# The end of a fused attention and gMLP kernel: flag read ahead of the last stage, last tile stored in one piece, output tiles finished beside every second step

## Chip, cores, metric

One core of one Trainium2 chip. The metric is the device time in microseconds (us), median over runs. Before: 1325.91 us (3 runs, 1325.71 to 1326.42); with three more runs 1325.83 us (6 runs, 1325.55 to 1326.42).

The profile's names: PE is TensorE, PEld its weight loads, DVE VectorE, ACT ScalarE, POOL GpSimd, SP SyncE; a q behind a name is the sequencer of that engine, under which the profile records its branches, semaphore waits and DMA issues. L1435 is line 1435 of the kernel; the lines after the change are numbered a little lower. Below, an engine's *silence* is the time from the end of its branch record to its next record, its *report* is the start of that next record, and a tile has *landed* where SP's wait record for it starts. *Fetch* is used for what fills a silence, as far as instruction packets in the DMA records show it. The records of these packets name a queue and no engine; they are given to engines here by size and order (in the changed kernel one of 16 KB starts 1.18 us after the start of TensorE's branch, one of 8 KB 1.02 us after DVE's and one 0.94 us after ACT's).

## The reference, cut to what matters

The whole computes adaLN modulation, attention with 32 query heads on a cached K and V of 8 heads, and a spatial-gating MLP. Only the last part is touched:

```python
z = gelu(einsum('bsd,df->bsf', h, w_in))
z1, z2 = z[..., :Fh], layernorm(z[..., Fh:])
g = einsum('ts,bsf->btf', w_sp, z2) + b_sp[None, :, None]
x = x + gb * einsum('bsf,fd->bsd', z1 * g, w_out)      # S = 2048, D = 512, Fh = 896
```

## The kernel before

The fast path computes softmax without subtracting the maximum and then sets `flag` to 0 if all sums were in a safe range. At its end every engine reads the flag into a register and jumps over `general_path`, a complete fallback program, if it is 0 (it is 0 for these inputs). The 2048 rows go in four chunks of 512. In the last chunk the gate is computed in two rounds of seven steps: columns 0 to 383 first, then the last 128 columns. Output tiles 0, 1, 2 of the chunk are complete at step 0 of the second round; tile 3 needs all seven steps.

```python
def finish_tile(t, jj, src, parts=1):
    j = t * CT + jj
    tmp = mlp.tile([P, D], FP32, name="tmp", bufs=2)
    yout = mlp.tile([P, D], BF16, name="yout", bufs=2)
    w = D // parts
    for k in range(parts):
        s = slice(k * w, (k + 1) * w)
        nc.vector.tensor_tensor(out=tmp[:, s], in0=src[:, s], in1=gb_rows[:, s], op=ALU.mult)
        nc.vector.tensor_tensor(out=yout[:, s], in0=tmp[:, s], in1=x_sb[:, j, s], op=ALU.add)
        (nc.scalar, nc.sync)[k].dma_start(out=out_dram[:, j, s], in_=yout[:, s])
# ... cut ...
acc = [bank2(), bank2()]                       # two PSUM tiles of 128 x 1024
o2_last = [acc[jj // 2][:, (jj % 2) * 512 : (jj % 2 + 1) * 512] for jj in range(CT)]
# ... first round, cut ...
for f in range(NFT):                           # second round, NFT = 7 steps
    spatial(last, yT, f, n_a, P, bias_by_pe=True)   # 16 matmuls, 1 bias matmul, 1 gate product on VectorE
    if f == 0:
        for jj in range(CT - 1):
            o2_mm(o2_last[jj], yT, jj, NFT - 1)
    else:
        o2_mm(o2_last[CT - 1], yT, CT - 1, f - 1)
    if 1 <= f < CT:
        finish_tile(last, f - 1, o2_last[f - 1])
o2_mm(o2_last[CT - 1], yT, CT - 1, NFT - 1)
finish_tile(last, CT - 1, o2_last[CT - 1], parts=2)
fast.close()

redo = nc.values_load(flag[0:1, 0:1], min_val=0, max_val=P)
with tc.If(redo != 0):
    general_path(...)
```

Of the kernel before, what the change touches and what calls it, by code (L numbers as in the profile page):

```python
# [13 lines left out]
ALU = mybir.AluOpType  # L14
AX = mybir.AxisListType
P = 128
# [559 lines left out]
def kernel(  # L576
# [19 lines left out]
    nc = tc.nc  # L596
    _, S, D = A_x.shape
# [12 lines left out]
    CT = 512 // P  # L610
# [8 lines left out]
    out_dram = out[0].rearrange("(t p) d -> p t d", p=P)  # L619
# [13 lines left out]
    flag = flagp.tile([1, 1], mybir.dt.int32, name="flag")  # L633
# [12 lines left out]
    x_sb = res.tile([P, NT, D], BF16, name="x_sb")  # L646
    ga_rows = res.tile([P, D], FP32, name="ga_rows")
    gb_rows = res.tile([P, D], FP32, name="gb_rows")
# [14 lines left out]
    def bank(name):  # L663
        return psum.tile([P, 512], FP32, name=name)
# [241 lines left out]
    for k in range(2):  # L906
        ln1_mod(hTs[0][:, k, 0:P], x_ps[0][:, k * P : (k + 1) * P], k)
        nc.scalar.activation(
            out=hTs[0][:, 2 + k, 0:P],
            in_=x_ps[1][:, k * P : (k + 1) * P],  # L910
# [17 lines left out]
    for hf, copy in enumerate((nc.vector.tensor_copy, nc.scalar.copy)):  # L928
        copy(  # L929
            out=qTs[0][:, 2 * hf : 2 * hf + 2, 0:P],  # L930
            in_=q_ps[:, hf * 512 : hf * 512 + 2 * P].rearrange("p (h q) -> p h q", h=2),
# [381 lines left out]
    for f in range(NFT):  # L1313
# [6 lines left out]
        out=ok1[:], in0=rall[:], scalar1=1.0 / SAFE, scalar2=None, op0=ALU.is_ge  # L1320
# [8 lines left out]
        out=bad[:], in0=okm[:], scalar1=-1.0, scalar2=1.0, op0=ALU.mult, op1=ALU.add  # L1329
# [12 lines left out]
    def spatial(t, yT, f, c0, n, bias_by_pe=False):  # L1342

        g_ps = bank("misc")
        cols = slice(t * 512 + c0, t * 512 + c0 + n)
        for st in range(NT):
            nc.tensor.matmul(  # L1347
                g_ps[:, :n],
                lhsT=z2[:, st, f * P : (f + 1) * P],
                rhs=wsp[t][:, st, c0 : c0 + n],  # L1350
                start=(st == 0),
                stop=(st == NT - 1 and not bias_by_pe),
            )
        if bias_by_pe:
            nc.tensor.matmul(  # L1355
                g_ps[:, :n], lhsT=ones_bf[0:1, :], rhs=bsp_bc[0:1, cols], start=False, stop=True
            )
            gbs = g_ps[:, :n]
        else:
            gb = mlp.tile([P, 512], BF16, name="gb", bufs=2)  # L1360
            gbs = gb[:, :n]
            nc.vector.tensor_tensor(out=gbs, in0=g_ps[:, :n], in1=bsp_bc[:, cols], op=ALU.add)  # L1362
        nc.vector.tensor_tensor(
            out=yT[:, f, c0 : c0 + n], in0=gbs, in1=z1T[:, f, cols], op=ALU.mult
        )

    def o2_mm(dst, yT, jj, f):
        nc.tensor.matmul(  # L1368
            dst,
            lhsT=yT[:, f, jj * P : (jj + 1) * P],  # L1370
            rhs=wout_sb[:, f, :],
            start=(f == 0),
            stop=(f == NFT - 1),
        )

    def finish_tile(t, jj, src, parts=1):
        j = t * CT + jj
        tmp = mlp.tile([P, D], FP32, name="tmp", bufs=2)
        yout = mlp.tile([P, D], BF16, name="yout", bufs=2)
        w = D // parts  # L1380
        for k in range(parts):
            s = slice(k * w, (k + 1) * w)
            nc.vector.tensor_tensor(out=tmp[:, s], in0=src[:, s], in1=gb_rows[:, s], op=ALU.mult)
            nc.vector.tensor_tensor(out=yout[:, s], in0=tmp[:, s], in1=x_sb[:, j, s], op=ALU.add)  # L1384
            (nc.scalar, nc.sync)[k].dma_start(out=out_dram[:, j, s], in_=yout[:, s])

    yTs = {}

    def o2_tile(t, jj):
        o2 = bank("o_ps")  # L1390
        for f in range(NFT):
            o2_mm(o2[:], yTs[t], jj, f)
        finish_tile(t, jj, o2)

    last = NCH - 1
    n_a = 512 - P
    for t in range(NCH):
        yTs[t] = mlp.tile([P, NFT, 512], BF16, name="yT", bufs=2)
        if t == last:
            break  # L1400
        for f in range(NFT):
            spatial(t, yTs[t], f, 0, 512)
            if t == 1 and f == CT:
                check_flag()
            if t > 0 and f < CT:
                o2_tile(t - 1, f)
        if t == 0:
            wsp[last] = wspp.tile([P, NT, 512], BF16, name="wsp")
            for st in range(NT):
                load_wsp(wsp[last], last, st)  # L1410
    acc = [bank2(), bank2()]
    o2_last = [acc[jj // 2][:, (jj % 2) * 512 : (jj % 2 + 1) * 512] for jj in range(CT)]
    yT = yTs[last]
    for f in range(NFT):
        spatial(last, yT, f, 0, n_a)
        if f < CT:
            o2_tile(last - 1, f)
        if f > 0:
            for jj in range(CT - 1):
                o2_mm(o2_last[jj], yT, jj, f - 1)  # L1420
    for f in range(NFT):
        spatial(last, yT, f, n_a, P, bias_by_pe=True)
        if f == 0:
            for jj in range(CT - 1):
                o2_mm(o2_last[jj], yT, jj, NFT - 1)
        else:
            o2_mm(o2_last[CT - 1], yT, CT - 1, f - 1)
        if 1 <= f < CT:
            finish_tile(last, f - 1, o2_last[f - 1])
    o2_mm(o2_last[CT - 1], yT, CT - 1, NFT - 1)  # L1430
    finish_tile(last, CT - 1, o2_last[CT - 1], parts=2)
    fast.close()

    redo = nc.values_load(flag[0:1, 0:1], min_val=0, max_val=P)
    with tc.If(redo != 0):  # L1435
        general_path(
            tc, A_x, A_k_cache, A_v_cache, A_wq, A_wo, B_x, B_w_in, B_w_sp, B_b_sp, B_w_out,
# [32 lines left out]
```

## Time and profile before

| kernel before | us | where it is read |
|---|---|---|
| device time, median | 1325.83 | 6 runs |
| span in the profile | 1324.6 | page |
| last bias matmul starts | 1316.09 | timeline, L1355 |
| last VectorE result ends | 1318.81 | timeline, L1384 |
| tail: last bias matmul to end of span | 8.47 | difference, with the end at 1324.56 in the trace |

The profile lines of the kernel before stand in the prediction.

### The profile page before, as it was taken

The numbers are of one execution on the slowest core, as the hardware profiler recorded it, in microseconds if no ns is written. First come the engines' busy times: TensorE is split into PE (matmuls) and PEld (weight loads), VectorE is DVE, ScalarE is ACT, GpSimd is POOL, SyncE is SP. The second block draws the span as 40 slices with busy tenths as digits, with TensorE's granted clock in tenths as the row PEclk, the third lists the DMA queues.
The fourth block names the chain that finished last, engine by engine and source line by source line (L and its number), as shares of the span: only waits on it lengthen the run. The fifth ranks groups of instructions, "written<-read, shape, count | busy, mean of one in ns | idle before, by whom it ended". The sixth has DMA issues, their size and how long they took to land.

```text
span 1324.6 us, 27877 instructions
## 1 busy us (share of the span) xinstructions
PE 1313.2 (99%) x12332; PEld 858.6 (65%) x12332; DVE 473.2 (36%) x1168; ACT 1077.8 (81%) x1061; POOL 49.4 (4%) x92
## 2 busy tenths in 40 slices
PE   8999999999999999999999999999999999999997
PEld 5666666666666666666666666666666666644444
DVE  5632222222222222222222222222222566793444
ACT  6898999999999999999999999999999999650000
POOL 1200000000000000000000000000000000120000
PEclk9999999999999999999999999999999999999999
DMA  7451022102111112111110221021101121143200
GB/s 179 123 122 33 13 49 37 37 13 53 28 26 33 34 37 37 30 36 37 33 37 14 53 37 33 17 52 24 31 13 21 25 34 33 29 116 83 64 21 27
DMA packets 148352, 58.12 MB, mean 44 GB/s; under 512 B 138400, under 2 KB 143904, under 8 KB 148224
## 3 DMA queue, kind: packets, MB, share of 16 engines
q1 hardware_dynamic: 141568, 37.84, 15.1%
q0 software_dynamic: 4208, 16.39, 4.4%
q10 hardware_dynamic: 2448, 2.03, 0.5%
q8 instruction: 98, 1.61, 0.5%
q14 instruction: 30, 0.25, 0.1%
HBM read 21.37 MB, written 2.10 MB: 18 GB/s over the span
## 4 chain that ended last, share of the span: by engine, by line
PE 98%; DMA 0%; DVE 0%; SPq 0%; issue 0%; ACT 0%
PE o_ps L1002 35%; PE s_ps L980 33%; PE misc L1034 8%; PE misc L947 8%; PE misc L1347 7%; PE s_ps L1193 2%; PE s_ps L1232 2%; PE o_ps L1368 1%; PE s_ps L1368 1%; DMA wq_g<-in_A_wq_dram 0%; PE misc L1104 0%; SPq L699 0%; PE misc L1355 0%; PE s_ps L921 0%; PE misc L846 0%; DVE yout L1384 0%
## 5 line engine op out<-in xcount | busy, mean ns | idle before, releaser
L987 ACT ACTIVATE pT<-s_ps 128x1024 bf16<-128x1024 f32 x1024 | 1044.5, 1025 | 83.4 <-PE s_ps L980 9.4
L1002 PEld LDWEIGHTS <-pT 128*128 128x128 bf16 x8192 | 548.5, 98 | 241.2
L1002 PE MATMUL o_ps<-v,pT 128*128 128x129 bf16 x8192 | 631.4, 220 | 0.0
L980 PE MATMUL s_ps<-qT,kT 128*128 128x512 bf16 x2048 | 609.9, 379 | 0.7 <-ACT qT L929 0.7
L1013 DVE RECIPROCAL rall<-o_ps 128x2 f32<-128x2 f32 x256 | 43.7, 171 | 744.4 <-PE o_ps L1002 744.2
L980 PEld LDWEIGHTS <-kT 128*128 128x128 bf16 x2048 | 199.5, 98 | 119.2 <-issue 1.4
L1034 PE MATMUL misc<-wo_g,oT 128*128 128x512 bf16 x512 | 194.0, 379 | 0.0
L947 PE MATMUL misc<-hT,wq_g 128*128 128x512 bf16 (+2 forms) x528 | 189.6, 371 | 0.0
L1014 DVE TENSOR_TENSOR onorm<-o_ps,rall 128x256 bf16<-128x256 f32 x256 | 108.7, 425 | 9.0 <-DVE rall L1013 0.3
L1347 PE MATMUL misc<-wsp,z 128*128 128x512 bf16 (+2 forms) x560 | 100.7, 336 | 0.0
L958 DVE CAST qT<-misc 128x512 bf16<-128x512 f32 x127 | 86.3, 680 | 2.0 <-PE misc L947 1.9
L1347 PEld LDWEIGHTS <-z 128*128 128x128 bf16 x560 | 50.6, 98 | 48.4
L1047 DVE TENSOR_TENSOR xacc<-misc,xacc 128x512 f32<-128x512 f32 x112 | 76.2, 680 | 0.0
L947 PEld LDWEIGHTS <-wq_g 128*128 128x128 bf16 x528 | 50.6, 98 | 1.1 <-issue 0.2
L1034 PEld LDWEIGHTS <-oT 128*128 128x128 bf16 x512 | 50.1, 98 | 0.8
L1362 DVE TENSOR_TENSOR gb<-misc,bsp_bc 128x512 bf16<-128x512 f32 (+1 forms) x28 | 18.4, 658 | 59.0 <-PE misc L1347 59.0
L1193 PE MATMUL s_ps<-win_sb,hT 128*128 128x448 bf16 x128 | 27.0, 352 | 0.0
L1203 ACT ACTIVATE z<-s_ps 128x896 bf16<-128x896 f32 x16 | 14.7, 917 | 14.9 <-PE s_ps L1193 14.9
L1232 PE MATMUL s_ps<-hT,win_sb 128*128 128x512 bf16 x112 | 24.5, 379 | 0.0
L1240 ACT ACTIVATE z1T<-s_ps 128x1024 bf16<-128x1024 f32 x14 | 14.3, 1024 | 10.0 <-PE s_ps L1232 9.1
L691 DVE BATCH_NORM_STATS2 bnst<-x_sb 128x6 f32<-128x512 bf16 x32 | 21.9, 683 | 0.5
L715 POOL DMA_DIRECT2D wq_g<-in_A_wq_dram x7 | 5.3, 753 | 420.9 <-PE misc L947 420.9
(86 smaller groups left out, 283.4 us busy)
## 6 DMA issues: line engine op xcount, KB each, us to landing
wq_g<-in_A_wq_dram POOLq DMA_DIRECT2D x7, 512.0 KB, 3.9
v<-in_A_v_cache_dram POOLq DMA_DIRECT2D x7, 512.0 KB, 7.1
wo_g<-in_A_wo_dram POOLq DMA_DIRECT2D x7, 512.0 KB, 4.8
oT<-onorm SPq DMA_TRANSPOSE x128, 2.4
wsp<-in_w_mod_dram POOLq DMA_DIRECT2D x1, 2048.0 KB, 10.4
out_dram<-yout ACTq DMA_DIRECT2D x15, 128.0 KB, 1.7
win_sb<-in_B_w_in_dram POOLq DMA_DIRECT2D x1, 1792.0 KB, 7.8
x_sb<-in_A_x_dram SPq DMA_DIRECT2D x3, 512.0 KB, 5.6
```

The costliest lines, as they stand in the source:

```text
L947: nc.tensor.matmul(ps[0][:, o0 : o0 + n], lhsT=wqs[g][:, dt, hh * DH : (hh + 1) * DH], rhs=hTs[ch][:, dt, c0 : c0 + n], start=(dt == 0), s ...
L958: nc.vector.tensor_copy(out=dst, in_=src)
L980: nc.tensor.matmul(s_ps[:, h * 512 : (h + 1) * 512].rearrange("p (r q) -> p r q", r=REP), lhsT=groups[g]["kT"][:, kt * P : (kt + 1) * P], ...
L987: nc.scalar.activation(out=pTs[u][:, 2 * i : 2 * i + 2, :], in_=s_ps[:].rearrange("p (k q) -> p k q", k=2), func=ACT.Exp, scale=inv_sqrt_dh,)
L1002: nc.tensor.matmul(o_ps[:, hh % 2, 0 : DH + 1], lhsT=pTs[u][:, kt, hh * P : (hh + 1) * P], rhs=groups[g]["v1"][:, kt, 0 : DH + 1], start=( ...
L1013: nc.vector.reciprocal(out=rall[:, c0 : c0 + 2], in_=o_ps[:, :, DH])
L1014: nc.vector.tensor_tensor(out=onorms[u][:, hh - 1 : hh + 1, :], in0=o_ps[:, :, 0:DH], in1=rall[:, c0 : c0 + 2].unsqueeze(2).to_broadcast([ ...
L1034: nc.tensor.matmul(X_ps[:], lhsT=oTs[u][:, hh, :], rhs=groups[g]["wo"][:, hh, :], start=(hh == 0), stop=(hh == REP - 1),)
L1047: nc.vector.tensor_tensor(out=xaccs[j][:], in0=X_ps[:], in1=xaccs[j][:], op=ALU.add)
L1193: nc.tensor.matmul(ps[0][:, hf * 512 : hf * 512 + FC], lhsT=h2Ts[j // CT][:, dt, (j % CT) * P : (j % CT + 1) * P], rhs=win_sb[:, dt, FH + ...
L1232: nc.tensor.matmul(ps[0][:, k * 512 : (k + 1) * 512], lhsT=win_sb[:, dt, f * P : (f + 1) * P], rhs=h2Ts[2 * ch2 + k][:, dt, :], start=(dt ...
L1347: nc.tensor.matmul(g_ps[:, :n], lhsT=z2[:, st, f * P : (f + 1) * P], rhs=wsp[t][:, st, c0 : c0 + n], start=(st == 0), stop=(st == NT - 1 a ...
```

## The change

Intent: take the reads of the flag off the end; give the last tile two long VectorE instructions in place of four short ones, and one store; spread the other three finishes so that VectorE does not fall behind TensorE (in the kernel before, a product and a finish took 1.54 us of VectorE at step 1, where TensorE's step took 1.37).

```diff
-    def finish_tile(t, jj, src, parts=1):
+    def finish_tile(t, jj, src):
-        w = D // parts
-        for k in range(parts):
-            ... tmp, yout by halves ...
-            (nc.scalar, nc.sync)[k].dma_start(out=out_dram[:, j, s], in_=yout[:, s])
+        nc.vector.tensor_tensor(out=tmp[:], in0=src, in1=gb_rows[:], op=ALU.mult)
+        nc.vector.tensor_tensor(out=yout[:], in0=tmp[:], in1=x_sb[:, j, :], op=ALU.add)
+        nc.scalar.dma_start(out=out_dram[:, j, :], in_=yout[:])
 ...
+    redo = nc.values_load(flag[0:1, 0:1], min_val=0, max_val=P)
     for f in range(NFT):
         spatial(last, yT, f, n_a, P, bias_by_pe=True)
 ...
-        if 1 <= f < CT:
-            finish_tile(last, f - 1, o2_last[f - 1])
+        if f % 2 == 1:
+            finish_tile(last, f // 2, o2_last[f // 2])
     o2_mm(o2_last[CT - 1], yT, CT - 1, NFT - 1)
-    finish_tile(last, CT - 1, o2_last[CT - 1], parts=2)
+    finish_tile(last, CT - 1, o2_last[CT - 1])
     fast.close()
-    redo = nc.values_load(flag[0:1, 0:1], min_val=0, max_val=P)
     with tc.If(redo != 0):
```

More of the change, by code (lines that the diff above doesn't have):

```diff
@@ L1379, in finish_tile @@
         yout = mlp.tile([P, D], BF16, name="yout", bufs=2)
-        w = D // parts
-        for k in range(parts):
-            s = slice(k * w, (k + 1) * w)
-            nc.vector.tensor_tensor(out=tmp[:, s], in0=src[:, s], in1=gb_rows[:, s], op=ALU.mult)
-            nc.vector.tensor_tensor(out=yout[:, s], in0=tmp[:, s], in1=x_sb[:, j, s], op=ALU.add)
-            (nc.scalar, nc.sync)[k].dma_start(out=out_dram[:, j, s], in_=yout[:, s])
+        nc.vector.tensor_tensor(out=tmp[:], in0=src, in1=gb_rows[:], op=ALU.mult)
+        nc.vector.tensor_tensor(out=yout[:], in0=tmp[:], in1=x_sb[:, j, :], op=ALU.add)
+        nc.scalar.dma_start(out=out_dram[:, j, :], in_=yout[:])
     yTs = {}
@@ L1392, in o2_tile @@
             o2_mm(o2[:], yTs[t], jj, f)
-        finish_tile(t, jj, o2)
+        finish_tile(t, jj, o2[:])
     last = NCH - 1
```

## The prediction

Three marked cuts in it take out statements about the hardware that no trace or run of this case shows; the 3.0 to 3.9 us behind the first cut are the silences after the branch, read from the trace of the kernel before.

> **What bounds the kernel now.** I read the page of the run first. TensorE is busy 99% of the 1324.6 us span and carries 98% of the chain that ended last, so most of the program is matmul time, and the diff touches none of it: no matmul, no elementwise instruction before the last chunk, no load is added or removed. The change can only act in the last stage and in what follows the last matmul. So I cut the end into stretches (start and end in us, their length, then busy time of PE, PEld, DVE, ACT, POOL with counts, granted clock, DMA share, GB/s).
>
> ```profile
> 1315.26:1316.33 1.07, 1.07 (x19) 0.90 (x15) 0.01 (x1) 0.00 (x0) 0.00 (x0) 1.00 0.18 58
> 1316.33:1318.81 2.48, 0.69 (x2) 0.10 (x2) 1.91 (x5) 0.00 (x0) 0.00 (x0) 0.95 0.00 0
> 1318.81:1324.60 5.79, 0.00 (x0) 0.00 (x0) 0.00 (x0) 0.00 (x0) 0.00 (x0) 0.50 0.15 37
> ```
>
> TensorE is full up to 1316.33. Then come 2.48 us in which VectorE works alone, and 5.79 us in which no engine computes. These 8.3 us, 0.6% of the span, are what the change plays for. Next the chain of waits through the first part (start, us, what):
>
> ```profile
> 1316.35 0.30 DVE yT L1363
> 1316.65 0.05 issue
> 1316.70 0.40 PE s_ps L1368
> 1317.10 0.02 issue
> 1317.13 0.44 DVE tmp L1383
> 1317.56 0.02 issue
> 1317.59 0.42 DVE yout L1384
> 1318.01 0.35 DVE tmp L1383
> 1318.36 0.02 issue
> 1318.38 0.43 DVE yout L1384
> ```
>
> The last gate product, one matmul, then four half-width VectorE instructions, ending at 1318.81. For the 5.79 us after it the chain has nothing, so I asked for the sequencers' records of the line of the branch (L1435) and of the flag read (L1434).
>
> ```profile
> L1435 SPq EVENT_SEMAPHORE  x8: 17/17/17, 1322.3 to 1322.9; - x8
> ...
> L1435 PEldq COMPARE_BRANCH  x1: 3927/3927/3927, 1317.3 to 1317.3; - x1
> L1435 ACTq COMPARE_BRANCH  x1: 54/54/54, 1319.0 to 1319.0; - x1
> L1435 DVEq COMPARE_BRANCH  x1: 72/72/72, 1319.1 to 1319.1; - x1
> L1435 SPq COMPARE_BRANCH  x1: 53/53/53, 1319.3 to 1319.3; - x1
> ...
> L1435 ACTq EVENT_SEMAPHORE  x1: 17/17/17, 1322.1 to 1322.1; - x1
> ```
> ```profile
> L1434 SPq TENSOR_LOAD <-flag x1: 474/474/474, 1242.4 to 1242.4; - x1
> ...
> L1434 PEldq TENSOR_LOAD <-flag x1: 488/488/488, 1316.7 to 1316.7; - x1
> L1434 DVEq TENSOR_LOAD <-flag x1: 584/584/584, 1318.4 to 1318.4; - x1
> L1434 ACTq TENSOR_LOAD <-flag x1: 475/475/475, 1318.4 to 1318.4; - x1
> ```
>
> Every engine that jumps over the fallback program is silent for about 3 us after its branch: ACT from 1318.97 to 1322.14, DVE 1319.06 to 1322.25, SP 1319.26 to 1322.31, PE 1317.29 to 1321.27. In that time the DMA records show instruction packets: one of 16 KB from 1318.87, three of 8 KB from 1319.88 to 1320.72. SP branches last, because it first has to issue the second half of the last tile (1318.83, 0.37 us). Both halves have landed by then (their last packets end at 1321.16), so the output is not what SP waits for. Only then does SP run a string of 20 semaphore waits, 8 at L1435 and 12 at the end of the program, 62 to 95 ns apart, from 1322.31 to its drain at 1323.68; the end barrier takes 0.88 us more. **The end is therefore: last VectorE result X = 1318.81, SP's issue and branch, about 3 us of silence, 1.37 us of waits one after another, 0.88 us of barrier.**
>
> [...] 3.0 to 3.9 us per engine with instruction packets in it; GpSimd, with little to skip, needs 0.18 us from its branch to its next record. [...] The trace shows the sequencer well ahead: a semaphore wait of L1034 was done at 467.98, and the weight load that follows it in the program started at 469.25, 14 weight loads later. [...] Here: 128x256 takes 0.42 us, 128x512 takes 0.69, so a pair of halves costs about 0.15 us more.
>
> **Part 1, the flag read moved ahead.** Removed from the end: one TENSOR_LOAD each on PE, ACT and DVE. On ACT the branch came 0.59 us after its DMA issue ended (1318.38 to 1318.97); without the read I take SP's 0.06 us. Added ahead of the last stage, near 1306: 0.49 us on PE's sequencer. TensorE then has three 512-column matmuls (0.65 us) and about ten 384-column ones (0.16 us each) queued, over 2 us by the look-ahead above, so I charge nothing. DVE's read (0.58 us) falls between its product at 1306.58 and the next at 1307.68, in which it idles 0.74 us. ACT is idle. SP and POOL had read the flag at 1242.4 already.
>
> **Part 2, the last tile in one piece on ACT's queue.** Four instructions become two. From the start of the first to the end of the last was 1318.81 - 1317.13 = 1.68 us. The full-width finish of this stage (below) takes from 1309.69 to 1310.41 + 0.69, 1.41 us: -0.27 us. The larger effect is not in the intent of the words: SP has no work left after its loads, so its branch should move to about 1243, beside GpSimd's, its 3 us of silence are then hidden, and it walks through its string of waits while the others still work. What it meets last is then a semaphore of the tile's landing or of ACT's last act.
>
> **Part 3, finishes after every second step.** Before, tiles 0, 1, 2 were finished at steps 1, 2, 3; now at 1, 3, 5. The finish of step 5 lies just ahead of the last gate product, which is on the path. How much it delays I read from step 1:
>
> ```profile
> 1309.48 0.29 DVE L1363 TENSOR_TENSOR yT<-misc,z1T 128x128 bf16<-128x128 f32 x1 [1.51 <-PE misc L1355]
> ...
> 1309.69 0.68 DVE L1383 TENSOR_TENSOR tmp<-s_ps,gb_rows 128x512 f32<-128x512 f32 x1
> 1310.41 0.69 DVE L1384 TENSOR_TENSOR yout<-tmp,x_sb 128x512 bf16<-128x512 f32 x1
> ...
> 1311.02 0.28 DVE L1363 TENSOR_TENSOR yT<-misc,z1T 128x128 bf16<-128x128 f32 x1
> ```
>
> From one product to the next with a finish between: 1.54 us. TensorE's step is 1.37 us (1309.22 to 1310.59 between bias matmuls). So the last product starts at 1314.98 + 1.54 = 1316.52 instead of 1316.35: **+0.17 us**. Steps 1 and 3 cost nothing, because the matmul that needs their successor comes a step later.
>
> **The sum.** Last product 1316.52; +0.35 matmul (as 1316.35 to 1316.70), +0.43 to the first finish instruction, +1.41: X' = 1318.71, against 1318.81. ACT issues at 1318.74, branches at 1319.14 (0.34 issue, 0.06), and after 0.05 + 3.12 us, its silence in the trace, reports at 1322.31. SP has meanwhile seen the landing: earlier whole tiles land in 1.7 us (median of the issues), so 1320.4, then 16 waits of about 0.065 us, 1321.5, before ACT. Last wait and drain 0.11 us, barrier 0.88: end at 1323.30, against 1324.6: **-1.3 us**. Nearly all of it is SP's string of waits taken out of the series (1.37 less 0.11), the flag reads and the tile giving 0.1 net on VectorE. On the measured time: 1325.91 - 1.3 = 1324.6.
>
> **Rivals.**
> 1. The flag read stalls TensorE, because its sequencer does not refill in time ahead of 128-column matmuls that pass every 56 ns. For it: the read waits in order in the same stream. Against: 14 pairs of look-ahead, 0.49 us. It would give back up to 0.5 us: 1325.1. I give it one in four.
> 2. The landing becomes the end. The two halves took 2.8 and 2.9 us, with instruction packets beside them. If the whole tile did too: 1318.74 + 2.9 + 1.05 + 0.11 + 0.88 = 1323.7, time 1325.0. Against: ACT's fetch begins about 0.85 us after its branch, near 1320.0, behind most of the tile's packets.
> 3. SP's branch stays late (its read of the flag placed behind something that waits): the string of waits returns to the series and only 0.1 to 0.5 us is gained, 1325.6. Against: nothing is left for it to wait on.
> 4. The end is slower, because the delay of 0.17 us grows, by a wait for an output buffer. Against: its two buffers are filled 2.7 us apart and land in 1.7.
>
> **Range and chances.** All rivals stay between 1323.8 and 1326. The three runs before spread over 0.7 us, and the new runs may be on another chip, so I take 1323.6 to 1325.9, with 1324.7 as the centre (1324.6, and something for rival 1). A change of 2% would need 26 us, three times all that lies behind the last full step: within 2% at 0.99.
>
> **What would show it.** Right: SP's branch near 1243; no flag read after 1310; the last gate product about 0.17 us later after its matmul sum; two 0.69 us finish instructions; ACT's record behind its branch at about 1322.3 and SP's drain within 0.2 us of it. Wrong: a gap in TensorE near 1306, SP's eight waits still starting after 1322, or a difference of several us, which could only come from the 1300 us that the diff does not touch.

## The result, and the profile after

The changed kernel takes 1324.13 us (6 runs, 1323.95 to 1325.52), 1.70 us less than 1325.83. The ratio is 0.9988 (95% interval 0.9976 to 1.0001). The ratio is the mean of one kernel's runs over that of the other's, so not quite the ratio of the medians quoted. Five of the six runs lie between 1323.95 and 1324.46; the slowest, 1325.52, happens to be the profiled one. Its weight loads stand 0.53 us later than those of the profile before at 5 us and 1.00 us later from 20 us on, long ahead of anything the diff touches. That offset is not counted as an effect of the change, and times of the two profiles must be compared after taking it off, or by tails.

| | before | after |
|---|---|---|
| last bias matmul to start of last gate product | 0.26 | 0.55 |
| last bias matmul to end of last VectorE result | 2.72 | 2.73 |
| from there to end of span | 5.75 | 3.92 |
| tail | 8.47 | 6.66 |

VectorE's part has gained nothing; all 1.82 us come from behind it. The stretches behind the last full step say the same (start and end, length, then busy time of PE, PEld, DVE, ACT, POOL, granted clock, DMA share, GB/s): 2.48 us of VectorE as before, then 3.92 us where 5.79 were (5.75 with the end of the span not rounded up).

```profile
1317.34:1319.82 2.48, 0.68 (x2) 0.10 (x1) 1.96 (x4) 0.00 (x0) 0.00 (x0) 1.00 0.19 59
1319.82:1323.74 3.92, 0.00 (x0) 0.00 (x0) 0.00 (x0) 0.00 (x0) 0.00 (x0) 0.63 0.15 46
```

The chain that ended last, after (start, us, what):

```profile
1315.78 0.49 PE misc L1355
...
1316.30 0.70 DVE tmp L1380
...
1317.02 0.69 DVE yout L1381
1317.71 0.21 DVE yT L1363
...
1317.97 0.40 PE s_ps L1368
...
1318.40 0.70 DVE tmp L1380
...
1319.12 0.69 DVE yout L1381
```

Now the finish of tile 2 (L1380, L1381 at 1316.30) is itself on the path, ahead of the last gate product (L1363). In the chain of before that product followed the matmuls directly.

The sequencers' records, first of the branch, then of the flag read:

```profile
L1432 SPq EVENT_SEMAPHORE  x8: 17/17/17, 1313.8 to 1321.9; - x8
...
L1432 SPq COMPARE_BRANCH  x1: 53/53/53, 1244.3 to 1244.3; - x1
L1432 PEldq COMPARE_BRANCH  x1: 3640/3640/3640, 1318.0 to 1318.0; - x1
L1432 DVEq COMPARE_BRANCH  x1: 72/72/72, 1319.1 to 1319.1; - x1
L1432 ACTq COMPARE_BRANCH  x1: 54/54/54, 1320.2 to 1320.2; - x1
...
L1432 ACTq EVENT_SEMAPHORE  x1: 17/17/17, 1322.8 to 1322.8; - x1
```
```profile
L1418 ACTq TENSOR_LOAD <-flag x1: 474/474/474, 1299.1 to 1299.1; - x1
L1418 PEldq TENSOR_LOAD <-flag x1: 489/489/489, 1304.7 to 1304.7; - x1
L1418 DVEq TENSOR_LOAD <-flag x1: 543/543/543, 1307.6 to 1307.6; - x1
```

SP branches at 1244.3 and its eight waits begin at 1313.8, while the stage still runs. It sees the last tile landed at 1321.65, 1.80 us after the issue at 1319.85, walks through 16 more waits and reaches the last one at 1322.69; ACT reports at 1322.77, SP drains at 1322.86, and the barrier takes 0.88 us as before. The waits from 1321 us on (the first five are the landing's and four more; the longest of the last twelve, 127 ns, is the last, which waits for ACT):

```profile
L1432 SPq EVENT_SEMAPHORE  x5: 17/17/17, 1321.7 to 1321.9; - x5
```
```profile
L1462 SPq EVENT_SEMAPHORE  x12: 27/28/127, 1322.0 to 1322.7; - x12
```

So most of the string still follows the landing; what it no longer follows is SP's own branch and silence, and it now runs beside ACT's. TensorE shows no delay from its flag read. The first bias matmul behind it, in the timelines of before and after, is later by the same 0.99 to 1.00 us as everything since 20 us:

```profile
1307.42 0.22 PE L1355 MATMUL misc<-bsp_bc,ones_bf 1*128 1x128 bf16 x1
```
```profile
1308.41 0.22 PE L1355 MATMUL misc<-bsp_bc,ones_bf 1*128 1x128 bf16 x1
```

### The profile page after: what moved, and what is told of

The parts are those of the page before. It is cut to its first block, busy times and chain, and to the rows that moved or that the text cites. A ratio compares the mean times of both kernels' runs of the same rounds, so it can differ in the third digit from the quotient of the medians. Undisturbed runs are those within 1.5% of the kernel's fastest.

```text
span 1323.7 us, 27668 instructions
## 1 busy us (share of the span) xinstructions
PE 1303.0 (98%) x12127; PEld 859.5 (65%) x12332; DVE 472.6 (36%) x1166; ACT 1077.6 (81%) x1061; POOL 48.9 (4%) x92
## 4 chain that ended last, share of the span: by engine, by line
PE 98%; issue 1%; DMA 0%; DVE 0%; SPq 0%; ACT 0%; ACTq 0%
PE s_ps L980 36%; PE o_ps L1002 35%; PE misc L947 7%; PE misc L1347 7%; PE misc L1034 6%; PE s_ps L1193 2%; PE s_ps L1232 2%; PE o_ps L1368 1%; PE s_ps L1368 0%; DMA wmod_a<-in_w_mod_dram 0%; PE misc L1104 0%; PE s_ps L921 0%; DVE tmp L1380 0%; DVE yout L1381 0%; PE misc L1355 0%
## 5 line engine op out<-in xcount | busy, mean ns | idle before, releaser
L947 PE MATMUL misc<-hT,wq_g 128*128 128x512 bf16 (+2 forms) x466 | 166.6, 370 | 0.1
L1034 PE MATMUL misc<-wo_g,oT 128*128 128x512 bf16 x386 | 146.3, 379 | 0.0
```

Of the source, the lines that this page charges most:

```text
L947: nc.tensor.matmul(ps[0][:, o0 : o0 + n], lhsT=wqs[g][:, dt, hh * DH : (hh + 1) * DH], rhs=hTs[ch][:, dt, c0 : c0 + n], start=(dt == 0), s ...
L1034: nc.tensor.matmul(X_ps[:], lhsT=oTs[u][:, hh, :], rhs=groups[g]["wo"][:, hh, :], start=(hh == 0), stop=(hh == REP - 1),)
```

## The experiments

Theory: the end was SP's late branch with its string of waits in series; the one-piece store on ACT frees SP, and this is most of the gain. Rivals: the flag reads paid, or the fewer VectorE instructions paid. Ten runs on three chips, with five rounds each; all outputs were correct. Times in us, each beside its own runs of the kernel before:

| run | time | beside before | change | tail |
|---|---|---|---|---|
| flag_only | 1325.39 | 1325.80 | -0.41 | 8.11 |
| piece_only | 1324.56 | 1325.80 | -1.24 | 6.95 |
| spread_only | 1325.74 | 1325.80 | -0.06 | 8.59 |
| steps_123 | 1323.71 | 1325.80 | -2.09 | 6.32 |
| last_on_sp | 1325.65 | 1325.56 | +0.09 | 8.19 |
| swap_banks | 1323.93 | 1325.56 | -1.63 | 6.60 |
| no_fallback | 1324.04 | 1325.56 | -1.52 | 5.68 |
| after_again | 1324.09 | 1325.83 | -1.74 | 6.65 |
| act_late | 1324.76 | 1325.83 | -1.07 | 7.56 |
| scaled_w | 1323.43 | 1325.83 | -2.40 | 5.74 |

By the 2% rule all are "same"; the larger differences between the tails tell them apart.

**One part alone: flag_only.**

```diff
+    redo = nc.values_load(flag[0:1, 0:1], min_val=0, max_val=P)   # ahead of the second round
-    redo = nc.values_load(flag[0:1, 0:1], min_val=0, max_val=P)   # behind the last finish
```

> Kernel before with the flag read moved ahead of the last stage and nothing else; tile in halves, finishes at steps 1, 2, 3. I measure the tail, from the start of the last bias matmul to the end of the span: before 8.47 us, after 6.66 us. My theory: SP still issues a half last, branches last and runs its 20 waits in series, so the tail stays at 8.0 to 8.5 us (a little shorter only if SP's silence shrinks because the other engines' fetches come earlier). Rival (the flag reads off ACT, DVE and PE are what paid): tail about 7.9 us or less, with SP's waits starting 0.5 us earlier. Rival (read stalls TensorE): a gap of up to 0.5 us in TensorE near the read. Measured time against before: 0 to -0.5 us.

Tail 8.11, -0.36 us, inside the range of the theory; the rival's 7.9 was not reached. SP's branch stands where it stood (3.18 us after the last bias matmul, both times); it is SP's silence that shrank, from 3.00 to 2.63 us. In the kernel before ACT, DVE and SP jump within 0.30 us of each other; here ACT and DVE jump 0.86 us ahead of SP. TensorE shows no gap.

**piece_only.**

```diff
-    finish_tile(last, CT - 1, o2_last[CT - 1], parts=2)
+    finish_tile(last, CT - 1, o2_last[CT - 1])
```

> Kernel before with the last tile in one piece on ACT's queue and nothing else; flag read at the end, finishes at steps 1, 2, 3. My theory (most of the gain is SP's branch and its waits leaving the series): SP branches near 1243, tail 6.9 to 7.5 us against 8.47, time -1.0 to -1.6 us. Rival (the gain is the flag read): tail 8.2 us, only the 0.27 us of fewer VectorE instructions. The span from the first finish instruction of the last tile to its last end: 1.68 to 1.41 us.

Tail 6.95, -1.52 us, of which 0.26 us are VectorE's (its last result 2.46 us after the bias matmul, against 2.72; the finish took 1.42 us, against 1.68). The records of the branch show SP gone early:

```profile
L1435 SPq EVENT_SEMAPHORE  x8: 17/17/17, 1312.9 to 1321.4; - x8
...
L1435 SPq COMPARE_BRANCH  x1: 53/53/53, 1243.3 to 1243.3; - x1
```

This is the largest of the parts. One thing came unlooked for: the tile landed only 2.48 us after its issue, against 1.80 in the changed kernel. With the flag reads at the end, DVE's 8 KB instruction packet (3.42 to 3.98 us after the bias matmul), with 0.04 us of TensorE's 16 KB one before it (to 3.37) and 0.07 us of ACT's behind it (from 4.36), overlap the tile's packets (3.33 to 4.44). For this reason or another, here the landing set the end and not ACT: SP came to its last wait 0.02 us after ACT's report.

**spread_only.**

```diff
-        if 1 <= f < CT:
-            finish_tile(last, f - 1, o2_last[f - 1])
+        if f % 2 == 1:
+            finish_tile(last, f // 2, o2_last[f // 2])
```

> Kernel before with the finishes at steps 1, 3, 5 and nothing else. My theory: the finish of tile 2 at step 5 delays the last gate product by 0.28 us (the size seen in the changed kernel, not the 0.17 us predicted), nothing else moves: tail 8.75 us, time +0.3 us. Rival (the spread relieves VectorE and gains): tail 8.4 us or less.

The last gate product starts 0.28 us later, as expected, and so does the last result (2.99 against 2.72 us after the bias matmul). The tail grows by 0.11 only, to 8.59, because SP's silence is 2.83 us here and not 3.00. A difference of 0.11 us between single profiles is not shown to be more than scatter, and the time, -0.06 us, shows neither. The spread alone gains nothing; the expected size was missed.

The three parts alone sum to -0.36 - 1.52 + 0.11 = -1.77 us of tail; together they gave -1.82. That the sum fits is partly luck: the flag read is worth 0.63 us and not 0.36 once the tile is in one piece, and the spread costs 0.33 and not 0.11 once both others are in (next run); the two differences nearly cancel.

**The spread undone: steps_123.** The changed kernel with the first two lines of the last diff in place of the last two.

> Changed kernel with the finishes put back to steps 1, 2, 3; flag early and tile in one piece stay. My theory: the last gate product is 0.28 us earlier, tail 6.35 to 6.45 us against 6.66, time 0.2 to 0.3 us under the changed kernel, the best of all. Rival (the end is set by something that does not follow the last product, as the fetch of another engine): tail stays 6.66 us.

Tail 6.32, 0.03 us under the expected range (ACT's silence was 2.45 us, in the changed kernel 2.50), time 1323.71: by 0.33 us of tail better than the changed kernel, and better than both kernels in time. Everything behind the last gate product moved with it, and the tile landed 1.83 us after its issue. Against piece_only, which lacks only the moved flag read, it gains 0.63 us: ACT's branch came 0.55 us earlier without the read in front of it, and the landing 0.65 us earlier. That the landing gained because fewer instruction packets stood in its way is read from the overlap and not shown by a run of its own.

**The store on the other queue: last_on_sp.** The changed kernel, same VectorE work, but (cut: `finish_tile` hands `queue` on to the store)

```diff
+    finish_tile(last, CT - 1, o2_last[CT - 1], queue=nc.sync)
-    finish_tile(last, CT - 1, o2_last[CT - 1])
```

> Changed kernel with the last tile still in one piece, but issued on SP's queue; flag early, finishes at steps 1, 3, 5. I measure the tail, from the start of the last bias matmul to the end of the span: before 8.47 us, after 6.66 us. My theory: SP now branches behind the issue, is silent 2.5 to 3.0 us and runs its 20 waits (1.37 us) in series again: tail 8.0 to 8.5 us, +1.3 to +1.8 us over the changed kernel, although VectorE's work is the same. Rival (which queue issues does not matter, the gain came from fewer and earlier instructions): tail 6.6 to 6.9 us.

Tail 8.19, +1.54 us; the time is that of the kernel before. One word, the queue of the last store, takes back 85% of the change's 1.82 us. The records:

```profile
L1432 SPq EVENT_SEMAPHORE  x8: 17/17/17, 1322.1 to 1322.6; - x8
...
L1432 SPq COMPARE_BRANCH  x1: 53/53/53, 1319.3 to 1319.3; - x1
...
L1432 ACTq EVENT_SEMAPHORE  x1: 17/17/17, 1320.0 to 1320.0; - x1
```

ACT is done at 1320.0 here, but SP begins its waits only at 1322.1, after a silence of 2.71 us behind its branch. The rival that it does not matter which queue issues has fallen.

**The delay of the last gate product: swap_banks.**

```diff
-    o2_last = [acc[jj // 2][:, (jj % 2) * 512 : (jj % 2 + 1) * 512] for jj in range(CT)]
+    o2_last = [acc[jj % 2][:, (jj // 2) * 512 : (jj // 2 + 1) * 512] for jj in range(CT)]
```

> Changed kernel with the accumulators paired so that output tile 2 shares its PSUM tile with tile 0, no longer with tile 3. My theory: the first finish instruction of step 5 waited 0.12 us for the matmul that wrote tile 3's half of the same PSUM tile; paired otherwise it starts 0.21 us after the gate product instead of 0.32, the last gate product is 0.12 us earlier, tail 6.54 us. Rival (the wait is the engine's own spacing): 0.32 us and tail 6.66 us as before.

In the changed kernel the finish of step 5 began 0.32 us after the gate product's start, right at the end of the matmul that wrote tile 3's half of the same PSUM tile; the chain above has that matmul's place at 1315.78 for 0.49 us (the record of the matmul itself is missing in the trace). The instruction's record carries a wait on TensorE's semaphore. Paired otherwise, from the timeline of swap_banks:

```profile
1314.44 0.29 DVE L1363 TENSOR_TENSOR yT<-misc,z1T 128x128 bf16<-128x128 f32 x1 [0.80 <-PE misc L1355]
...
1314.64 0.68 DVE L1380 TENSOR_TENSOR tmp<-s_ps,gb_rows 128x512 f32<-128x512 f32 x1
...
1315.97 0.28 DVE L1363 TENSOR_TENSOR yT<-misc,z1T 128x128 bf16<-128x128 f32 x1
```

0.21 us, and 1.53 us from product to product, which is the predicted 1.54; in the changed kernel it was 1.66. The record of this instruction no longer has the wait; that of tile 1's finish at step 3, which now shares with tile 3, has it instead, and starts 0.32 us after its product. So it is a wait that the program itself contains for the shared tile. The last result came 0.13 us earlier. The tail gained 0.06 only, where 0.12 had been expected: the tile landed 1.97 us after its issue this time, not 1.80, and SP's string from there ended after ACT's report (its last wait at 5.65 us behind the bias matmul, ACT at 5.60).

**No jump at all: no_fallback.** The changed kernel without `with tc.If(redo != 0): general_path(...)`; right only because the flag is 0 on these inputs.

> Changed kernel without the branch and the fallback program (right on these inputs only, because the flag is 0 here; an experiment, no candidate). No engine jumps. My theory: the landing of the last tile (1.8 us after its issue) and SP's waits behind it end within 0.1 us of ACT's fetch, so removing every fetch gains only 0 to 0.5 us: tail 6.2 to 6.66 us. Rival (ACT's 2.5 us of fetch alone sets the end): tail near 4.5 us.

Tail 5.68: both expectations missed. The landing is nearly where it was (1.74 us after the issue, not 1.80), so removing every fetch did not bring the end near 4.5. But SP's string changed too: from the landing on it has five wait records instead of 17, and the stretch from the landing to SP's drain is 0.31 us instead of 1.20.

```profile
L1457 SPq EVENT_SEMAPHORE  x5: 27/28/28, 1321.3 to 1321.5; - x5
```

Twelve records at 0.065 us are 0.78 us, the wait for ACT another 0.1. The run takes away fetch and waits together, so it does not say what each costs alone. In the changed kernel they run side by side and end 0.08 us apart; by these records (an estimate) without ACT's fetch alone the end would come 0.1 us earlier, without the twelve waits alone not at all. The median of the time (-1.52 us) doesn't show the 0.98 us of tail against the changed kernel; its five runs spread from 1322.74 to 1324.98. The profiled run (1324.21) lost 0.67 us to the kernel before in its first 10 us, which the tail leaves out; for the other four it stays open.

**The changed kernel once more, and ACT alone delayed: after_again, act_late.**

> The changed kernel as it is, once more, beside the two others of this call on one chip. Tail (start of the last bias matmul to the end of the span) 6.6 to 6.7 us, time about 1324.1 us, -1.5 to -1.8 us against before.

Tail 6.65, time -1.74 us: as before.

```diff
     finish_tile(last, CT - 1, o2_last[CT - 1])
+    nc.values_load(flag[0:1, 0:1], engines=[mybir.EngineType.Activation], min_val=0, max_val=P)
```

> Changed kernel with one more read of the flag on ACT alone, behind its last DMA issue and ahead of its branch; it is used for nothing. It delays only ACT's branch, by the 0.55 us that such a read took in the kernel before; landing and SP's string stay where they are. My theory (ACT's fetch and SP's string end within 0.1 us of each other, so either one, delayed, moves the end): SP's last wait ends 0.4 to 0.6 us later, waiting for ACT; tail 7.1 to 7.25 us. Rival (landing and SP's string alone set the end, with room beside them): tail stays 6.65 us.

Tail 7.56, +0.91 us, time +0.67 us over after_again on the same chip. ACT's branch came 0.63 us later and its silence was 2.78 us, where 2.50 had been expected, so the size is over the range, and why the silence grew stays open; the direction is the theory's. SP reached its last wait at the usual place, 5.59 us after the last bias matmul (5.63 in after_again), and stood there until ACT reported at 6.59: that report and the end of the span both moved by 0.91 us.

```profile
L1435 ACTq EVENT_SEMAPHORE  x1: 17/17/17, 1322.2 to 1322.2; - x1
```
```profile
SPq L1465 <- ACTq L1435: 1.1, 1, 1.1
```

So ACT's fetch bounds the changed kernel, and SP's string, at 0.08 us from it (0.05 in after_again), would be next.

**A shorter finish: scaled_w.** From steps_123; the last tile's output weights are multiplied by the gate row beforehand, into a buffer that is free by then.

```diff
+            if t == 2:
+                nc.vector.tensor_tensor(
+                    out=wout_g[:, f, :], in0=wout_sb[:, f, :], in1=gb_rows[:], op=ALU.mult)
 ...
-    finish_tile(last, CT - 1, o2_last[CT - 1])
+    yout = mlp.tile([P, D], BF16, name="yout", bufs=2)
+    nc.vector.tensor_tensor(out=yout[:], in0=o2_last[CT - 1], in1=x_sb[:, NT - 1, :], op=ALU.add)
+    nc.scalar.dma_start(out=out_dram[:, NT - 1, :], in_=yout[:])
```

> Steps 1, 2, 3 (the best so far, tail 6.32 us), and the gate row multiplied into a copy of the output weights during the third chunk, where VectorE has room, for the last output tile alone; its finish is then one addition instead of a product and an addition. My theory (everything behind the last VectorE result follows it): that result comes 0.72 us earlier, and of this 0.1 to 0.7 us reaches the end, less than all because the tile's packets move into the time of TensorE's 16 KB instruction packet and may land later: tail 5.6 to 6.25 us. Rival (the end is held by TensorE's fetch, which starts no earlier): tail 6.3 us. Time 0.1 to 0.7 us under steps 1, 2, 3.

The last result came 0.73 us earlier (1.73 us after the bias matmul), the tail is 5.74, 0.58 us under steps_123. The landing took 2.00 us, and SP's string behind it, not ACT, ended last. Time 1323.43, -2.40 us against before, the best usable version measured.

## Why the prediction was right, and where it was not

**The central step held.** SP's branch went to 1244.3 and its string of waits ran beside ACT's silence instead of behind its own. This accounts for most of the gain: piece_only -1.52 us of tail (0.26 of it VectorE's), and last_on_sp, which puts only SP's lateness back, +1.54.

**The sum was too small.** Predicted -1.3 us; measured -1.70 in the medians and -1.82 in the tails. The mis-sized term is ACT's silence after its branch, taken over as 3.12 us; it was 2.50, and the 0.11 us that VectorE lost (below) stands against that. In the kernel before, three engines jumped within 0.30 us and their 8 KB packets overlapped; in the changed kernel ACT jumps alone, 1.08 us behind DVE. Six profiles in which ACT jumps alone show 2.45 to 2.54 us; where jumps come close together or near TensorE's packet it was 2.63 to 3.13. But ACT in act_late, 1.71 us behind DVE, had 2.78, and SP in last_on_sp, 1.13 us behind DVE, 2.71. That company lengthens the fetch is therefore a pattern with exceptions, not shown by an experiment of its own; why ACT's silence shrank stays open.

**Part 3 was mis-sized.** The last gate product was delayed by 0.28 us, not 0.17. The neglected 0.12 us is the wait for tile 3's matmul in the shared PSUM tile; I had read the spacing from step 1, where tile 0 shares with tile 1 and no such matmul is under way. swap_banks gave the predicted spacing back. With this, VectorE's part came to +0.01 us instead of -0.10: the spread ate what the single piece had gained.

**Part 1 had too small a share.** "Nearly all of it is SP's string" is not what the runs show: the flag read alone brings 0.36 us, by SP's shorter silence, and 0.63 us once the tile is in one piece (piece_only against steps_123). The prediction's own sum held most of this without naming it: ACT's branch 0.06 us behind its issue, where with the read it came 0.59 behind. A smaller slip of reading: the waits of SP's string stand 59 to 95 ns apart, not 62 to 95.

**Rival 1** (TensorE stalls on its flag read) did not happen: no delay beyond the constant 1.00 us. **Rival 2** (the landing becomes the end) was much nearer than "before ACT" by 0.8 us: SP's string came to its last wait 0.08 us ahead of ACT, because ACT's silence was shorter than assumed and the landing 0.2 us later; in act_late ACT is shown to bound. In piece_only, swap_banks and scaled_w, where the tile took 1.97 to 2.48 us to land, the landing did become the end. **Rival 3** is last_on_sp, by another road, and would have cost what it named. **Rival 4** came true in half: the end was not slower, but the delay of 0.17 us did grow, by a wait that I had not named, not for an output buffer but for a PSUM tile.

## What to carry to other kernels

At the end of a program look past the last compute instruction: which sequencer jumps last, what it fetches, and how many waits it then walks through one after another (in the kernel before SP: 3.00 us of silence, then 20 waits in 1.37 us); give the last store to a queue whose engine has the fewest duties afterwards (here ACT's against SP's: 1.54 us of tail in last_on_sp; GpSimd's queue was not tried). Finishing work spread "evenly" was not free here, because the last piece stood in front of a product on the path and waited for a matmul that wrote the other half of its PSUM tile (both undone in steps_123: 0.33 us of tail; the wait alone in swap_banks: the last result 0.13 us earlier). To judge changes of one or two us in a run of a thousand, measure from a late fixed event, not the whole time, and profile each version more than once, which was done here for one only.

## What the runs show of branches, reads, waits and landings

- After the taken branch the silence was 2.45 to 3.13 us on ACT, DVE and SP; on PE it was 3.45 to 3.99 us from the start of the branch to the next record. The instruction packets have 16,384 bytes behind TensorE's jump and 8,192 bytes behind those of ACT, DVE and SP.
- The flag read (TENSOR_LOAD), one value from an on-chip tile, took 0.47 to 0.58 us (0.29 for act_late's extra one), and the one in the stream of TensorE caused no delay that the trace shows: the first bias matmul behind it was later by the same 0.99 to 1.00 us as everything since 20 us.
- The records of the branch are 45 to 72 ns on ACT, DVE, SP and GpSimd, and 3.39 to 3.93 us on PE, where the fetch lies inside the record (in the kernel before, the 16 KB packet from 1318.87 to 1319.83 in a record from 1317.29 to 1321.21).
- SP walks through 20 waits at the end of the kernel before, 59 to 95 ns apart, 1.37 us in all. From the last landing on there are 17 in the changed kernel and five without the branch.
- Whether instruction packets delay stores is suggested by the runs and not isolated: the last 128 KB tile landed in 1.74 and 1.79 us without overlap (no_fallback, act_late), in 1.80 to 1.84 us with at most 0.06 us of it, in 1.97 and 2.00 us with 0.15 to 0.2 us (swap_banks, scaled_w), and in 2.48 us with 0.67 us (piece_only); the halves before, 64 KB each, took 2.8 and 2.9 us.
